# Loading the first two row tiles of x as one transfer, with the third on another queue and one short warming matmul less

## The chip, the cores and the metric

The kernel runs on one core of one Trainium2 chip. The metric is the device time of one execution in microseconds (us), and the median of several runs is compared. Three runs of the kernel before gave 220.68, 220.12 and 220.95 us: a median of 220.68.

## The reference

One layer norm feeds two blocks that are added to the input: a linear attention with a softmax feature map (32 heads of 16), and a gated unit with a plain product.

```python
x  = A_x                                   # 2048 x 512, bf16
xn = layernorm(x)                          # no gain, no bias
# block A
q, k, v = heads(xn @ A_wqkv)               # 32 heads of 16
phi(t)  = concat(softmax(t @ w_phi), softmax(-(t @ w_phi)))
kv, z   = phi(k)^T v, sum over rows of phi(k)
a = (phi(q) kv) / (phi(q) z + 1e-6) @ A_wo
# block B
h = (xn @ B_w_gate) * (xn @ B_w_up)        # 2048 x 1792
b = h @ B_w_down
out = x + a + b
```

## The kernel before

The 2048 rows are cut into 16 tiles of 128 rows; `xall` holds all of them, 512 columns each. `xnT` is the normalised x with its columns on the partitions, as TensorE wants it for every product that follows. The weights stay in SBUF: `wv` (the v part of `A_wqkv`, loaded in two halves), `wg` and `wu` (gate and up, loaded in column stretches), `wT2` (the k and q parts, transposed by the transfer), `wd`, `wo`.

The order of the work on each engine is the order in which the code is written; no scheduler changes it. So each engine's list and each queue's list of transfers can be read off the code:

- SyncE's queue starts with x tile 0 (L82), x tile 2 (L83) and the second half of `wv` (L84). Then come the first columns of `wg` and `wu` (L94), `wphi`, more of `wg` and `wu`, the transposing load of `wT2` and the rest.
- ScalarE's queue carries x tile 1 (L91) and the first half of `wv` (L92). GpSimd's carries x tile 3 (L93).
- Transfers from SyncE and ScalarE signal on eight semaphores in turn, and a transfer that comes round to a semaphore again waits until the transfer that used it last has landed.

The first four tiles have a path of their own, since nothing can run before them (L376 to L405). For tile 0, VectorE sums the rows (`sum_of(0)`, L374); for tiles 1 and 2 ScalarE does it with an accumulating pass into `junk` (L378); for tile 3 VectorE again. `sub_sum` (L338) makes 512 x minus the row sum on VectorE, for tile 0 in two halves, and calls it `xn`. `lt` (L206, L207) transposes `xn` by four TensorE matmuls against the identity, into a PSUM tile `tp`, and copies it to `xnT` on VectorE or ScalarE. `first_v` (L237) multiplies with `wv`; its results for tiles 0 and 1 go to `kv` banks, those of tiles 2 and 3 to `pv`. The scale by the standard deviation is applied later, when PSUM is read (L364, L362), from statistics that VectorE takes after the sums (L154, L343).

Behind that, TensorE alternates between units of the gated block (`ffn`: four matmuls `g`, four `u`), the k, q and v projections, the attention's products and the last product `fin`. Ahead of it all, TensorE runs matmuls on a constant that nobody reads, `warm_up`: seven of 512 columns (L312) and two of 128 columns (L313).

Of the kernel before, what the change touches and what calls it, by code (L numbers as in the profile page):

```python
# [21 lines left out]
def kernel(  # L22
# [12 lines left out]
    nc = tc.nc  # L35
# [32 lines left out]
    def dma_x(lo, hi, eng=nc.sync):  # L68
        eng.dma_start(out=xall[:, lo:hi, :], in_=x_view[:, lo:hi, :])
# [4 lines left out]
    def dma_wv(lo, hi, eng):  # L74
        eng.dma_start(out=wv[:, lo:hi, :],
                      in_=A_wqkv[lo * P:hi * P, 2 * D:3 * D].rearrange("(c p) f -> p c f", p=P))
# [2 lines left out]
        dma_cols(nc.sync, wg, B_w_gate, lo, hi)  # L79
        dma_cols(nc.sync, wu, B_w_up, lo, hi)  # L80

    dma_x(0, 1)  # L82
    dma_x(2, 3)  # L83
    dma_wv(2, DC, nc.sync)  # L84

    ET = mybir.EngineType
# [1 line left out]
    ones = nc.const_aps.tensor(1.0, [P, P], BF16)  # L88
    first = consts.tile([P, 1], BF16)
    nc.scalar.activation(out=first[:], in_=ones[:, 0:1], func=AF.Exp, scale=1.0)  # L90
    dma_x(1, 2, nc.scalar)  # L91
    dma_wv(0, 2, nc.scalar)  # L92
    dma_x(3, 4, nc.gpsimd)  # L93
    dma_gu(0, 2 * P)  # L94
# [212 lines left out]
    def warm_up(k, reps=DC):  # L307
        for _ in range(k):
            nc.tensor.matmul(warm[:, 0:reps * P], lhsT=ones,
                             rhs=nc.const_aps.tensor(1.0, [P, reps * P], BF16), start=True, stop=True)  # L310

    warm_up(7)  # L312
    warm_up(2, 1)  # L313

    with tc.tile_pool(name="ps_k", bufs=1, space=PSUM) as ps_k:
        kvbank = [ps_k.tile([P, TT], F32, name=f"kv{b}") for b in range(2)]
# [209 lines left out]
```

## Time and profile before

| | us |
|---|---|
| median of the three runs | 220.68 |
| lowest, highest run | 220.12, 220.95 |
| the profiled execution | 220.46 |
| its span | 218.8 |
| TensorE busy in the span | 214.9 |
| VectorE busy | 141.0 |
| ScalarE busy | 89.2 |
| GpSimd busy | 74.9 |

The span runs from the profile's first event to its last; the profiled execution took 1.66 us more than its span. Times inside the span below are counted from its start. In a timeline row the first number is the start, the second the length of the row, in us; rows of like instructions are merged, with their count after the x, and PEld is TensorE's weight load. A matmul's length contains the way through the array and overlaps with the next one's, so the pace of TensorE is read from the distance between starts. In the rows of transfers the last number is the time from the issue to the landing.

### The profile page before, as it was taken

The numbers are of one execution on the slowest core, as the hardware profiler recorded it, in microseconds if no ns is written. First come the engines' busy times: TensorE is split into PE (matmuls) and PEld (weight loads), VectorE is DVE, ScalarE is ACT, GpSimd is POOL, SyncE is SP. The second block draws the span as 40 slices with busy tenths as digits, with TensorE's granted clock in tenths as the row PEclk, the third lists the DMA queues.
The fourth block names the chain that finished last, engine by engine and source line by source line (L and its number), as shares of the span: only waits on it lengthen the run. The fifth ranks groups of instructions, "written<-read, shape, count | busy, mean of one in ns | idle before, by whom it ended". The sixth has DMA issues, their size and how long they took to land.

```text
span 218.8 us, 3493 instructions
## 1 busy us (share of the span) xinstructions
PE 214.9 (98%) x1291; PEld 103.1 (47%) x1291; DVE 141.0 (64%) x242; ACT 89.2 (41%) x159; POOL 74.9 (34%) x72
## 2 busy tenths in 40 slices
PE   8999999999999999999999999999999999999994
PEld 3444445454444444444544444444444444454443
DVE  4878867786598758576599773296655655454321
ACT  5545686569575875565435212141231322100000
POOL 4450843373357554636045333033123033000000
PEclk9999999999999999999999999999999999999999
DMA  5999996005202240202028355114461431412201
GB/s 198 286 297 372 372 219 136 2 0 51 48 0 49 51 94 2 48 3 48 1 43 105 76 114 114 37 24 96 96 70 30 95 72 28 96 48 72 69 30 48
DMA packets 48433, 19.91 MB, mean 91 GB/s; under 512 B 37504, under 2 KB 48384, under 8 KB 48416
## 3 DMA queue, kind: packets, MB, share of 16 engines
q1 hardware_dynamic: 47952, 19.16, 38.9%
q10 hardware_dynamic: 416, 0.39, 0.5%
q8 instruction: 10, 0.16, 0.3%
q0 software_dynamic: 48, 0.13, 0.2%
q14 instruction: 7, 0.06, 0.1%
HBM read 8.67 MB, written 2.10 MB: 49 GB/s over the span
## 4 chain that ended last, share of the span: by engine, by line
PE 97%; DMA 1%; DVE 1%; issue 0%
PE g L275 22%; PE fin L291 22%; PE u L279 22%; PE fin L294 6%; PE q L237 6%; PE k L237 6%; PE pv L237 6%; PE kv L331 2%; PE ab L465 2%; DMA xall<-in_A_x_dram 1%; PE kv L237 1%; PE tp L206 1%; PE pq L226 1%; DVE tot L374 0%; DVE xn L338 0%; DVE o_sb L301 0%
## 5 line engine op out<-in xcount | busy, mean ns | idle before, releaser
L275 PE MATMUL g<-xnT,wg 128*128 128x512 bf16 x224 | 57.5, 379 | 0.0
L279 PE MATMUL u<-xnT,wu 128*128 128x512 bf16 x224 | 57.5, 379 | 0.0
L254 POOL TENSOR_TENSOR phiq<-e,rsum 128x1024 bf16<-128x1024 f32 x16 | 30.9, 1933 | 63.5 <-DVE rsum L252 56.0
L283 DVE TENSOR_TENSOR hT<-u,g_sb 128x512 bf16<-128x512 f32 x56 | 37.0, 666 | 23.9 <-PE u L279 15.8
L282 ACT CAST g_sb<-g 128x512 bf16<-128x512 f32 x56 | 32.9, 587 | 46.8 <-PE g L275 46.5
L250 DVE TENSOR_REDUCE sums<-e 128x64 f32<-128x1024 f32 x32 | 38.9, 1216 | 20.1 <-ACT e L247 20.1
L291 PE MATMUL fin<-wd,hT 128*128 128x512 bf16 (+2 forms) x238 | 51.1, 366 | 0.0
L254 POOL TENSOR_TENSOR phik<-e,rsum 128x1024 bf16<-128x1024 f32 x16 | 30.9, 1932 | 39.6 <-DVE rsum L252 33.6
L279 PEld LDWEIGHTS <-wu 128*128 128x128 bf16 x224 | 21.9, 98 | 26.4
L291 PEld LDWEIGHTS <-hT 128*128 128x128 bf16 x238 | 22.4, 98 | 24.8
L275 PEld LDWEIGHTS <-wg 128*128 128x128 bf16 x224 | 21.1, 98 | 24.0
L237 PEld LDWEIGHTS <-xnT 128*128 128x128 bf16 x192 | 17.4, 98 | 18.2 <-ACT xnT L207 0.7
L301 DVE TENSOR_TENSOR o_sb<-fin,xall 128x512 bf16<-128x512 f32 (+2 forms) x13 | 8.5, 651 | 20.5 <-PE fin L294 20.5
L252 DVE RECIPROCAL rsum<-sums 128x64 f32<-128x64 f32 x32 | 17.7, 553 | 3.1
L294 PE MATMUL fin<-wo,oT 128*128 128x512 bf16 (+2 forms) x68 | 16.6, 366 | 0.0
L237 PE MATMUL k<-W1k,xnT 128*128 128x512 bf16 x64 | 16.4, 379 | 0.0
L237 PE MATMUL q<-W1q,xnT 128*128 128x512 bf16 x64 | 16.4, 378 | 0.0
L246 ACT ACTIVATE e<-q 128x512 f32<-128x512 f32 x12 | 7.2, 597 | 22.2 <-PE q L237 22.2
L237 PE MATMUL pv<-wv,xnT 128*128 128x512 bf16 x56 | 14.4, 379 | 0.0
L478 DVE TENSOR_TENSOR otok<-ab,rden 128x512 bf16<-128x512 f32 x16 | 11.1, 692 | 0.6
L323 ACT CAST vt<-pv 128x512 bf16<-128x512 f32 x12 | 7.0, 587 | 10.0 <-PE pv L237 10.0
L154 DVE BATCH_NORM_STATS2 stats<-xall 128x6 f32<-128x512 bf16 x16 | 10.6, 664 | 0.0
(63 smaller groups left out, 131.8 us busy)
## 6 DMA issues: line engine op xcount, KB each, us to landing
out_dram<-o_sb SPq DMA_DIRECT2D x15, 128.0 KB, 2.0
wd<-in_B_w_down_dram SPq DMA_DIRECT2D x1, 1792.0 KB, 15.8
xall<-in_A_x_dram SPq DMA_DIRECT2D x1, 1024.0 KB, 11.9
wg<-in_B_w_gate_dram SPq DMA_DIRECT2D x1, 640.0 KB, 7.7
wu<-in_B_w_up_dram SPq DMA_DIRECT2D x1, 640.0 KB, 10.4
xall<-in_A_x_dram SPq DMA_DIRECT2D x1, 512.0 KB, 4.5
wg<-in_B_w_gate_dram SPq DMA_DIRECT2D x1, 512.0 KB, 5.3
wu<-in_B_w_up_dram SPq DMA_DIRECT2D x1, 512.0 KB, 6.4
```

The lines of the kernel that those rows point to most:

```text
L154: nc.vector.bn_stats(out=stats[:], in_=xall[:, n, :])
L237: nc.tensor.matmul(ps, lhsT=xnT[:, j, n * P:(n + 1) * P], rhs=w[:, j, :], start=(j == 0), stop=(j == DC - 1))
L250: nc.vector.tensor_reduce(out=sums[:], in_=ev, axis=AX.X, op=ALU.add)
L252: nc.vector.reciprocal(out=rsum[:].rearrange("p a b -> p (a b)"), in_=sums[:])
L254: nc.gpsimd.tensor_tensor(out=phi[:].rearrange("p g (x f) -> p (g x) f", f=DH), in0=ev, in1=rsum[:].to_broadcast((P, 2 * H, DH)), op=ALU.mult)
L275: nc.tensor.matmul(gps, lhsT=wg[:, c, f * P:(f + 1) * P], rhs=xnT[:, c, T * TT:(T + 1) * TT], start=(c == 0), stop=(c == DC - 1))
L279: nc.tensor.matmul(ups, lhsT=wu[:, c, f * P:(f + 1) * P], rhs=xnT[:, c, T * TT:(T + 1) * TT], start=(c == 0), stop=(c == DC - 1))
L282: nc.scalar.copy(out=g_sb[:], in_=gps)
L283: nc.vector.tensor_tensor(out=hTs[T][:, f, :], in0=ups, in1=g_sb[:], op=ALU.mult)
L291: nc.tensor.matmul(ps, lhsT=hTs[T][:, f, t4 * P:(t4 + 1) * P], rhs=wd[:, f, lo:lo + w], start=(f == 0), stop=False)
L294: nc.tensor.matmul(ps, lhsT=oTs[n][:, c, :], rhs=wo[:, c, lo:lo + w], start=False, stop=(c == DC - 1))
L478: nc.vector.tensor_tensor(out=o_tok[:].rearrange("p (b h d) -> p b h d", b=2, d=DH), in0=abv[:, :, :, 0:DH], in1=rden[:].to_broadcast((P, ...
```

## The change

x tiles 0 and 1 are asked for by one instruction on SyncE's queue (256 KB in place of 128 KB), tile 2 moves from SyncE's queue to ScalarE's, into the place that tile 1 had there, and the second of the two short warming matmuls is dropped. Lines from 84 on move up by one.

```diff
@@ -79,8 +79,7 @@
-    dma_x(0, 1)
-    dma_x(2, 3)
+    dma_x(0, 2)
     dma_wv(2, DC, nc.sync)
@@ -88,7 +87,7 @@
     nc.scalar.activation(out=first[:], in_=ones[:, 0:1], func=AF.Exp, scale=1.0)
-    dma_x(1, 2, nc.scalar)
+    dma_x(2, 3, nc.scalar)
     dma_wv(0, 2, nc.scalar)
     dma_x(3, 4, nc.gpsimd)
@@ -310,7 +309,7 @@
     warm_up(7)
-    warm_up(2, 1)
+    warm_up(1, 1)
```

Nothing else moves: each compute engine's list is as before, but for the one warming matmul and its weight load on TensorE. Both the sum of tile 0 on VectorE and the sum of tile 1 on ScalarE now wait for the one transfer. There is one transfer less in the turn of the eight semaphores, so every later transfer on SyncE's queue waits for another one than before.

## The prediction

> **What bounds the kernel now.** I read the page first (busy times, the slices, the chain's shares), then the chain of waits in order of time, then the timeline of the first 6 us, then the rows of transfers.
>
> The page's busy times, the granted clock in slices, and the chain's shares:
>
> ```profile
> PE 214.9 (98%) x1291; PEld 103.1 (47%) x1291; DVE 141.0 (64%) x242; ACT 89.2 (41%) x159; POOL 74.9 (34%) x72
> ...
> PEclk9999999999999999999999999999999999999999
> ...
> PE 97%; DMA 1%; DVE 1%; issue 0%
> ```
>
> TensorE (PE) is the bound, and 97% of the chain that ends last is its own work. The change touches none of that work, only when it starts. So the head of the chain decides (start, length, what):
>
> ```profile
> 0.79 2.45 DMA xall<-in_A_x_dram
> 3.25 0.02 issue
> 3.27 0.70 DVE tot L374
> 3.97 0.03 issue
> 3.99 0.30 DVE xn L338
> 4.29 0.05 issue
> 4.34 1.07 PE tp L206 x8
> 5.40 0.54 PE kv L237 x2
> 5.94 0.22 PE tp L206 x4
> ```
>
> The reader is to see that tile 0's landing at 0.79 + 2.45 = 3.24 sets the first real TensorE instruction at 4.34: 1.10 us of sum, subtraction and hand-overs lie between. From 4.34 on the chain never leaves TensorE again until the last output.
>
> The timeline of the same stretch, and of the issue queues:
>
> ```profile
> 0.83 3.36 PE L309 MATMUL warm<-const-bfloat16-1.0 128*128 128x512 bf16 x9 [0.83 <-PEq L510]
> 0.85 0.40 ACTq L69 DMA_DIRECT2D xall<-in_A_x_dram  x1
> 1.28 0.45 ACTq L75 DMA_DIRECT2D wv<-in_A_wqkv_dram  x1
> ...
> 3.57 0.63 ACT L378 ACTIVATE junk<-xall 128x512 bf16<-128x512 bf16 x1 [1.28 <-DMA xall<-in_A_x_dram]
> 3.77 0.15 PEld L309 LDWEIGHTS <-const-bfloat16-1.0 128*128 128x128 bf16 x1 [0.28 <-issue]
> ...
> 3.99 0.75 DVE L338 TENSOR_SCALAR xn<-xall,tot 128x256 bf16<-128x256 bf16 x3
> 4.11 0.19 ACT L378 ACTIVATION_READ_ACCUMULATOR junk<-xall 128x1 f32 x1
> ```
>
> The nine warming matmuls start 0.43 us apart when they are long and 0.11 when short; the last one starts at 3.88, so TensorE is free from 3.99 and stands idle for 0.35 us until 4.34. Two more readings of the starts matter. The eight transposes go from 4.34 to 5.20, 0.107 each, and the four at 5.78 take 0.055 each: TensorE runs at half pace at first, although the page's clock row shows full in all slices. And the first two `kv` matmuls start at 5.20 and 5.56. At 0.427 for a slow one and 0.216 for a fast one (four `g` take 0.86), a distance of 0.36 means 0.29 us of slow pace: full pace came at about 5.49, 4.66 us after the first warming matmul.
>
> **The change part by part.** *Tiles 0 and 1 in one transfer.* Its landing T isn't in the trace. The rows of transfers give the bounds:
>
> ```profile
> wv<-in_A_wqkv_dram ACTq DMA_DIRECT2D x1, 256.0 KB, 3.4
> ...
> xall<-in_A_x_dram ACTq DMA_DIRECT2D x1, 128.0 KB, 2.7
> ```
>
> From below: T is 3.24, if the second 128 KB cost nothing. From above: the first half of `wv` has the new transfer's size and shape and took 3.4 us, behind other transfers, so T = 0.79 + 3.4 = 4.19. Nearest is the pair itself: asked for at 0.79 and 0.85 on two queues, tile 1 was in when ScalarE began on it at 3.57. The same 256 KB beside the same neighbours, plus 0.03 us for the longer issue (`wv`'s 0.43 against 0.40): T = 3.60, and d = T - 3.24 = 0.36 us. A second way agrees: from 2.6 to 3.6 us all transfers together moved 343 to 379 GB/s, and 131 KB at 360 GB/s are 0.36 us.
>
> The Trainium skill ("DMA: Bandwidth & Descriptors", section "Anatomy of one DMA") fits 2.0 us plus the bytes at 436 GB/s, for GpSimd's queue. By it tile 0 alone takes 2.30 us, where the trace has 2.45, and d would be 0.30.
>
> *What tile 0's lateness does.* VectorE is the carrier: sum 3.27, the halves of tile 0's `xn` from 3.99 and 4.19, tile 1's `xn` from 4.40, then copies; these follow each other with no idle time named in the timeline. All of it moves by d, the first transpose to 4.34 + 0.36 = 4.70.
>
> *What tile 1's landing does.* It comes at 3.60 in place of 3.57. Its sum on ScalarE was ready at 4.11 + 0.19 = 4.30 and will be at 4.33; tile 1's `xn` could not start before 4.40 anyway, and now starts near 4.76. No gain, no loss: VectorE's order covers 0.43 us.
>
> *Tile 2 on ScalarE's queue* is issued at 0.85 in place of about 1.2. It lands near tile 1's old time, 3.6, in place of about 3.9. Its sum comes second on ScalarE, at 4.33 before, behind tile 1's, so it is not earlier; its `xn` stands at 5.19 in VectorE's list. Nothing, and if it were as late as 4.19 it would still be ahead of its turn. The `wv` half behind it keeps its place at 1.28 and landed at 4.68, ahead of its use at 5.20.
>
> *SyncE's queue* has one issue less of about 0.46 us. The second half of `wv` (issued 1.71, landed 4.4 later, at 6.1, needed at 6.96), `wg` (2.18 + 4.9 = 7.1, needed at 9.34) and `wu` (2.70 + 5.4 = 8.1, needed at 10.20) go out earlier and were not waited for. The waits for another semaphore in turn concern the later stretches: the second `wu` now waits for the new transfer (in by 4.19 at the latest, and it was issued at 4.36), the transposing load for `wv`'s second half, as before. GpSimd's queue isn't passed. Zero; without this cover the loss per transfer is what it comes late.
>
> *One short warming matmul less.* It frees 0.11 us of TensorE in which TensorE waits anyway: zero by itself. Together with d the idle hole grows from 0.35 us (3.99 to 4.34) to 0.82 us (3.88 to 4.70).
>
> *The sum.* From the first transpose on TensorE is the bound, so d passes to the end, but the work moved past 5.49 runs at twice the pace. Before, 4.34 to 5.49 did 1.15 us of slow work, worth 0.575 us of fast; after, 4.70 to 5.49 does 0.395. The end moves by 0.575 - 0.395 = 0.18 us. If full pace comes later by d as well, or if VectorE's shifted list (tile 2's `xn` would end at 5.53 + 0.36 = 5.89, its transpose came at 5.78) is what TensorE waits for, the end moves by all 0.36. I take 0.25, between the two, with 0 (d = 0) and 0.95 (T = 4.19, nothing regained) as ends. Against the profiled execution: 220.46 + 0.25 = 220.7. That execution lies 0.22 under the median of the runs shown, so the forecast for the median is 220.68 + 0.25 = 220.9 us.
>
> **The rivals.** *The hole keeps TensorE slow for longer* (slower). Speaking for it: full pace came only after 4.66 us of activity, and the hole in it more than doubles. Speaking against: 0.35 us of hole did no such harm. If the change of pace counts anew from the first transpose, full pace comes at 4.70 + 4.66 = 9.36. Slow work until then is worth 2.33 us of fast, and the end moves by (9.36 - 2.33) - (5.49 - 0.575) = 2.1 us: 222.6 on the profiled execution, 222.8 on the median. It decides only between 0.35 and 0.82 us of hole.
>
> On this the Trainium skill ("TensorE: Matmul & The Clock Gate", Part 1) says that half pace is the default, that one busy window of about 3.4 us ends it, and that the windows run freely, whatever the kernel does. By it a window that the larger hole spoils costs another 3.4 us at half pace, 1.7 us in the end, an estimate, and the executions scatter by as much; the three runs shown, 0.83 us apart, don't contradict it.
>
> *The second 128 KB cost nothing* (not slower). T = 3.24; for it speaks that the transfers moved only 87 to 128 GB/s before 2.4 us, so the start is latency and not rate; against it, that tile 1 on another queue came 0.33 us after tile 0. Then VectorE starts as before and nothing moves: 220.46, 220.7 on the median. It can't be faster: the earlier sum of tile 1 waits for VectorE's turn.
>
> *The merged transfer is as late as the half of `wv`.* T = 4.19, d = 0.95, first transpose at 5.29. By the sum above the end moves by 0.48 to 0.95: 221.2 to 221.6 on the median. Against it: `wv` stood behind two x tiles.
>
> **How the numbers follow.** Forecast 0.55, longer slow pace 0.24, no cost 0.11, late landing 0.10. A measurement of this kernel can tell about 0.5% from no change, 1.1 us. The forecast, no cost and late landing stay within 219.6 to 221.8; the longer slow pace lies beyond. Slower by over 0.5%: 0.27, that rival and a little of the late landing. Faster: even full pace from the first transpose at 4.34 would save only 0.575 us, so 0.04 for what I don't see. Within: 0.69. The forecast's own range is 220.4 to 221.3, a fourth of a microsecond for T and the rest for the scatter of the runs; the range goes from 220.2 into the rival's, to 222.6, which leaves out its upper half and little below.
>
> **What would show it.** The merged transfer's landing (3.6), the sum at 3.6, the first transpose at 4.7, a hole of 0.8 us ahead of it, and where the starts of matmuls go from 0.43 to 0.22 apart: near 5.5 if I am right, 8 or later for the first rival. I am wrong if the first transpose starts at 4.4 or earlier, or if TensorE stands idle later than 7 us, which would mean a transfer that I called covered.

## The result, and the profile after

| | kernel before | changed kernel |
|---|---|---|
| median of 22 runs | 220.69 us | 222.18 us |
| lowest, highest | 220.08, 222.73 | 220.75, 223.12 |
| runs above 221.8 us | 1 of 22 | 14 of 22 |
| profiled execution | 220.46 us | 222.47 us |
| its span | 218.8 us | 220.7 us |

The ratio of the times is 1.0054, with a 95% interval of 1.0033 to 1.0075: the changed kernel is slower by about half a per cent. The runs of the changed kernel fall into two groups, eight from 220.75 to 221.42 and fourteen from 221.99 to 223.12, with nothing between. The profiled execution belongs to the upper one.

The page of the changed kernel still shows TensorE as the bound. The lines are the busy times of the engines and the chain's shares by engine:

```profile
PE 214.9 (97%) x1266; PEld 103.5 (47%) x1290; DVE 141.1 (64%) x242; ACT 89.2 (40%) x159; POOL 75.0 (34%) x72
...
PE 96%; DMA 1%; issue 1%; DVE 1%
```

TensorE's busy time reads the same 214.9 us in a span that is 1.9 us longer, but the two can't be compared: this page has 1266 matmuls beside 1290 weight loads, so 24 matmuls are missing from the record, where the page of the kernel before has 1291 of each. A later profile of the changed kernel that belongs to the lower group has the same 1266 matmuls and 213.1 us. So between these two like profiles the upper one has 1.8 us more of busy time: the time lost is slow work and not waiting. The chain of waits of the changed kernel, in order of time (start, length, what), shows where that comes from in its first 10 us:

```profile
0.80 3.19 DMA xall<-in_A_x_dram
3.98 0.02 issue
4.01 0.70 DVE tot L373
4.71 0.02 issue
4.73 0.30 DVE xn L337
5.03 0.05 issue
5.07 1.07 PE tp L205 x8
6.14 0.85 PE kv L236 x2
6.99 0.43 PE tp L205 x4
7.42 0.85 PE kv L236 x2
8.27 0.85 PE pv L236 x2
9.13 0.56 PE kv L236 x2
9.69 0.22 PE tp L205 x4
9.91 0.43 PE kv L236 x2
```

Two things are to be seen. The merged transfer lands at 0.80 + 3.19 = 3.99 in place of 3.24, and the first transpose comes at 5.07 in place of 4.34, 0.73 us later. And two `kv` or `pv` matmuls take 0.85 us until 9.1, then 0.43: TensorE runs at half pace until about 9.3, where the kernel before had full pace at 5.49. The second is the larger by far. From 5.07 to 9.3 at half pace, TensorE does 2.1 us worth of fast work, so the end moves by (9.3 - 2.1) - (5.49 - 0.575) = 2.3 us by the prediction's sum; the two profiled executions lie 2.0 apart.

The timeline of the changed kernel shows the hole ahead of the first transpose (PE is TensorE; the bracket is its idle time and what ended it):

```profile
0.83 3.25 PE L308 MATMUL warm<-const-bfloat16-1.0 128*128 128x512 bf16 x8 [0.83 <-PEq L509]
...
5.07 1.07 PE L205 MATMUL tp<-ident,xn 128*128 128x128 bf16 x8 [0.99 <-DVE xn L337]
```

The bracket counts 0.99 us from the modelled end of the last warming matmul. By starts, as in the prediction, the hole goes from 3.88 to 5.07: 1.19 us. All holes below are counted by starts.

### The profile page after: what moved, and what is told of

Same layout as the page of the kernel before. It is cut to its first block, busy times and chain, and to the rows that moved or that the text cites. A ratio compares the mean times of both kernels' runs of the same rounds, so it can differ in the third digit from the quotient of the medians.

```text
span 220.7 us, 3465 instructions
## 1 busy us (share of the span) xinstructions
PE 214.9 (97%) x1266; PEld 103.5 (47%) x1290; DVE 141.1 (64%) x242; ACT 89.2 (40%) x159; POOL 75.0 (34%) x72
## 4 chain that ended last, share of the span: by engine, by line
PE 96%; DMA 1%; issue 1%; DVE 1%
PE u L278 22%; PE fin L290 22%; PE g L274 22%; PE fin L293 6%; PE q L236 6%; PE k L236 6%; PE pv L236 6%; PE ab L464 2%; PE kv L330 2%; DMA xall<-in_A_x_dram 1%; PE kv L236 1%; PE tp L205 1%; PE pq L225 1%; DVE tot L373 0%; DVE xn L337 0%
## 5 line engine op out<-in xcount | busy, mean ns | idle before, releaser
L278 PE MATMUL u<-xnT,wu 128*128 128x512 bf16 x221 | 56.8, 379 | 0.2
L274 PE MATMUL g<-xnT,wg 128*128 128x512 bf16 x213 | 56.3, 379 | 0.6
L236 PE MATMUL k<-W1k,xnT 128*128 128x512 bf16 x61 | 15.8, 379 | 0.0
L477 DVE TENSOR_TENSOR otok<-ab,rden 128x512 bf16<-128x512 f32 x16 | 11.1, 691 | 0.6
```

Source lines behind the costliest of these rows:

```text
L236: nc.tensor.matmul(ps, lhsT=xnT[:, j, n * P:(n + 1) * P], rhs=w[:, j, :], start=(j == 0), stop=(j == DC - 1))
L274: nc.tensor.matmul(gps, lhsT=wg[:, c, f * P:(f + 1) * P], rhs=xnT[:, c, T * TT:(T + 1) * TT], start=(c == 0), stop=(c == DC - 1))
L278: nc.tensor.matmul(ups, lhsT=wu[:, c, f * P:(f + 1) * P], rhs=xnT[:, c, T * TT:(T + 1) * TT], start=(c == 0), stop=(c == DC - 1))
L477: nc.vector.tensor_tensor(out=o_tok[:].rearrange("p (b h d) -> p b h d", b=2, d=DH), in0=abv[:, :, :, 0:DH], in1=rden[:].to_broadcast((P, ...
```

## The experiments

The theory after the result: the hole between the warming matmuls and the first transpose spoils the change to full pace in part of the executions, and the late landing costs little by itself. Its rivals: the late landing costs the time; the dropped warming matmul does. In each list of runs, those above 221.8 us are called the upper group; the kernel before, in its 22 runs above and beside each group of experiments, has 13 of 132 there. Kernels that were run together on one chip are told of together. The first four:

**The changed kernel with its hole filled.**

```diff
-    warm_up(1, 1)
+    warm_up(12, 1)
```

> The changed kernel with twelve short warming matmuls in place of one, so that TensorE stays busy until the first transpose at about 5.07. Theory (the hole of 1.19 us between 3.88 and 5.07 makes most executions stay at half pace until 8 us or later): the first transpose still starts near 5.05 to 5.1, full pace comes before 6.5, no execution lies at 222 or above, median 220.8 to 221.2. Rival (the late landing alone costs the time, and the hole does nothing): median 222.2, as the changed kernel, with full pace near 9 again.

Measured: median 221.22 us (220.61 to 221.64, 12 runs), none in the upper group; 220.85 for the kernel before beside it, ratio 1.0011 (0.9990 to 1.0031). Its timeline on TensorE from 3 us on:

```profile
2.49 2.77 PE L308 MATMUL warm<-const-bfloat16-1.0 128*128 128x512 bf16 x15
5.05 1.06 PE L205 MATMUL tp<-ident,xn 128*128 128x128 bf16 x8
5.90 0.89 PE L236 MATMUL kv<-wv,xnT 128*128 128x512 bf16 x2
6.63 0.39 PE L205 MATMUL tp<-ident,xn 128*128 128x128 bf16 x4
6.86 0.59 PE L236 MATMUL kv<-wv,xnT 128*128 128x512 bf16 x2
```

The first transpose is as late as in the changed kernel, 5.05, but the four transposes from 6.63 to 6.86 already go at 0.055 us each: full pace by 6.6. The late landing alone does not make the upper group. The median is at the upper edge of what was expected, 0.37 us above the kernel before.

**The hole without the late landing.**

```diff
-    warm_up(7)
+    warm_up(5)
     warm_up(2, 1)
```

> The kernel before with five long warming matmuls in place of seven: x lands as before, at 3.24, but TensorE is idle from about 3.18 to 4.34, a hole of 1.16 us. Theory (the hole): the first transpose is where it was, but part of the executions keeps half pace until 7.5 to 10 us; two groups, 220.1 to 221.0 and 221.4 to 222.6, median above 221.0. Rival (late landing alone): nothing moves, median 220.7 and all executions below 221.1.

Measured: median 222.42 us (221.37 to 224.25, 12 runs), nine of 12 in the upper group; ratio 1.0080 (1.0048 to 1.0112). This is more than the theory asked for: even the lowest run is 1.2 us above the lowest of the kernel before beside it. Its timeline on TensorE from 3 us on:

```profile
4.25 1.07 PE L206 MATMUL tp<-ident,xn 128*128 128x128 bf16 x8 [0.92 <-DVE xn L338]
6.07 1.01 PE L237 MATMUL kv<-wv,xnT 128*128 128x512 bf16 x2 [0.74 <-DMA wv<-in_A_wqkv_dram]
6.87 0.63 PE L206 MATMUL tp<-ident,xn 128*128 128x128 bf16 x4
7.30 1.06 PE L237 MATMUL kv<-wv,xnT 128*128 128x512 bf16 x2
...
9.28 0.39 PE L206 MATMUL tp<-ident,xn 128*128 128x128 bf16 x4
```

The first transpose is even earlier than in the kernel before, at 4.25, yet the transposes at 6.87 still take 0.107 each (to 7.30), and only those at 9.28 are fast. Two long warming matmuls less cost as much as the whole change in the first 22 runs (1.57 and 1.49 us in the medians). The second row has something else that the prediction denied: TensorE waits for the first half of `wv`, until 6.02 (more on it below).

**The transfers of the changed kernel alone.**

```diff
-    warm_up(1, 1)
+    warm_up(2, 1)
```

> The changed kernel with its second short warming matmul back: the transfers of the changed kernel alone, hole 1.08 us. Theory (the hole, made by the landing at 3.99): as the changed kernel, merged transfer in at about 3.99, first transpose near 5.07, two groups, median 221.7 to 222.3. Rival (the dropped warming matmul does it): median below 221.2. Rival (late landing alone): 222.2 in one group.

Measured: median 221.97 us (220.50 to 224.56), five runs from 220.50 to 221.28 and the others from 221.91 up; the ratio 1.0022 (0.9985 to 1.0060) can't be told from the kernel before. Two groups, as the changed kernel has them, so the dropped warming matmul isn't needed for them. Its profiled execution, 221.91, is in the upper group for another reason. Its chain:

```profile
1.29 5.58 DMA wv<-in_A_wqkv_dram
6.88 0.04 issue
6.92 0.59 PE kv L236 x2
7.51 0.22 PE tp L205 x4
```

The first half of `wv` landed at 6.88, 1.5 us later than in the changed kernel's own profile (1.29 + 4.1 = 5.39); the pace was full by then.

**One warming matmul less alone.**

```diff
-    warm_up(2, 1)
+    warm_up(1, 1)
```

> The kernel before with one short warming matmul less and its own transfers: hole 0.46 us in place of 0.35. Theory (the hole, and it has to be large): 220.5 to 220.9, same as before. Rival (the dropped warming matmul does it): 221.5 or above.

Measured: median 220.90 us (220.27 to 221.40, 11 runs), none in the upper group, ratio 0.9992 (0.9969 to 1.0015). As expected: a hole that is 0.1 us longer than the one of the kernel before did nothing that can be seen in 11 runs. (In its profiled execution x came early, VectorE began at 3.03, so the hole was only 0.22 us there.)

The next three ran together on another chip.

**Why the merged transfer came at 3.99: all on SyncE's queue.**

```diff
     dma_x(0, 2)
+    dma_x(2, 3)
+    dma_wv(0, 2, nc.sync)
     dma_wv(2, DC, nc.sync)
...
-    dma_x(2, 3, nc.scalar)
-    dma_wv(0, 2, nc.scalar)
```

> The changed kernel with ScalarE's queue left empty: tile 2 and the first half of wv follow the merged transfer on SyncE's queue. It settles why the merged transfer came at 3.99 and not at 3.60. Theory (the transfers of two queues take turns, so tile 2 on ScalarE's queue took bandwidth from the merged transfer): it lands at 3.3 to 3.55. Rival (256 KB in one transfer take this long by themselves): 3.75 to 4.0 as in the three runs with the merge so far. The time isn't the question, since the first half of wv comes later.

Measured: 221.18 us in the median (220.81 to 223.09, 10 runs, three in the upper group), ratio 1.0003 (0.9960 to 1.0046). The rows of its transfers (KB, us from issue to landing):

```profile
xall<-in_A_x_dram SPq DMA_DIRECT2D x1, 256.0 KB, 2.8
...
xall<-in_A_x_dram SPq DMA_DIRECT2D x1, 128.0 KB, 2.6
```

The merged transfer took 2.8 us from its issue at 0.79, and VectorE began on it at 3.63. With tile 2 on ScalarE's queue beside it, five profiled executions have VectorE begin at 4.01, 3.86, 3.78, 3.84 and 3.94. That is between the bounds of the theory and the rival, nearer the theory: without tile 2 beside it the transfer is 0.15 to 0.38 us faster, in one execution.

That execution, 223.09, is in the upper group for a third reason. Its row of the granted clock and its timeline on TensorE:

```profile
PEclk9699999999999999999999999999999999999999
...
2.49 1.39 PE L308 MATMUL warm<-const-bfloat16-1.0 128*128 128x512 bf16 x4
4.70 0.86 PE L205 MATMUL tp<-ident,xn 128*128 128x128 bf16 x8 [0.81 <-DVE xn L337]
6.55 0.65 PE L236 MATMUL kv<-wv,xnT 128*128 128x512 bf16 x2 [1.00 <-DMA wv<-in_A_wqkv_dram]
6.99 0.63 PE L205 MATMUL tp<-ident,xn 128*128 128x128 bf16 x4
7.42 1.06 PE L236 MATMUL kv<-wv,xnT 128*128 128x512 bf16 x2
...
10.39 0.59 PE L236 MATMUL kv<-wv,xnT 128*128 128x512 bf16 x2
```

By the starts, full pace came during the warming already, at 3.55. TensorE then stood idle for 0.81 us ahead of the first transpose and for 1.00 us ahead of `wv`, and at 6.97 it went back to half pace (the two `kv` from 7.42 take 1.06, those from 10.39 take 0.59) until 10.38. The clock row shows this as a 6 in its second slice, from 5.5 to 11.1 us. So full pace can also be lost again.

**A hole of the size that the prediction expected.**

```diff
-    warm_up(7)
+    warm_up(6)
     warm_up(2, 1)
```

> The kernel before with six long warming matmuls in place of seven: a hole of about 0.78 us (3.56 to 4.34), the size that the prediction expected of the change. Theory (a hole spoils the more executions, the larger it is): between the 0.46 us hole, which did nothing, and the 1.16 us hole, 222.4: median 221.0 to 221.9, with part of the executions above 221.5. Rival (a threshold between 0.8 and 1.1 us): median 220.9 and no more executions above 221.5 than the kernel before has.

Measured: median 220.90 us (220.42 to 222.93, 12 runs): seven runs from 220.42 to 220.98, five from 221.96 up; ratio 1.0008 (0.9970 to 1.0046). The median is the rival's, the five of 12 are the theory's; the kernel before had six of 29 in the upper group beside it, so the share is larger but not clear of chance. In its profiled execution, 222.93, the hole was 0.66 us, since x came a little earlier, and TensorE waited another 0.49 us for `wv`. The upper group lies where larger holes put it: its middle run is at 222.39, and the middle of the changed kernel's upper group is at 222.47.

**The kernel before with its hole filled.**

```diff
-    warm_up(2, 1)
+    warm_up(5, 1)
```

> The kernel before with five short warming matmuls in place of two, which closes its own hole of 0.35 us. Theory (a hole this small does no harm): median within 0.2 us of the kernel before; the few executions of the kernel before above 222 may vanish if they are holes' work. Rival (each bit of hole costs): median lower by 0.2 to 0.4 us, 220.5.

Measured: median 220.90 us (220.29 to 221.21, 12 runs), none in the upper group; ratio 0.9990 (0.9962 to 1.0018). The median doesn't move; no run is in the upper group, where the kernel before had six of 29 beside it (this too is not clear of chance in 12 runs).

**The first half of `wv` ahead of its second half**, on a further chip, with the hole filled and without:

```diff
     dma_x(0, 1)
-    dma_x(2, 3)
+    dma_wv(0, 2, nc.sync)
     dma_wv(2, DC, nc.sync)
...
     dma_x(1, 2, nc.scalar)
-    dma_wv(0, 2, nc.scalar)
+    dma_x(2, 3, nc.scalar)
...
-    warm_up(2, 1)
+    warm_up(5, 1)
```

> The kernel before with tile 2 and the first half of wv exchanged between the two queues (SyncE: tile 0, both halves of wv; ScalarE: tiles 1 and 2) and five short warming matmuls in place of two. The profiles so far show the first half of wv landing anywhere from 4.68 to 6.9, and TensorE waiting for it for up to 1.2 us, which the prediction called covered. Theory (its second half, on the other queue, takes turns with it; behind it in one queue it can't): it lands by 5.0, TensorE doesn't wait for it, full pace before 6.5, and the median is 0.2 to 0.5 us below the kernel before. Rival (its landing has other causes): it lands at 5.5 or later, median as the kernel before.

> As the last one, with the two short warming matmuls of the kernel before: the transfers alone. Theory (queues take turns): as the last one within 0.1 us in the median, since a hole of 0.35 us does little, but with one execution in ten or so above 222. Rival: as the kernel before.

Measured: filled 220.93 us (220.72 to 221.44, 12 runs), ratio 1.0000 (0.9987 to 1.0014); with the hole of the kernel before, 220.90 (220.66 to 223.10), two of 12 in the upper group, ratio 1.0014 (0.9988 to 1.0040). The landing came nearly as expected, at 5.25 in the filled one, where TensorE began with `wv` at 5.30, 0.1 us after its transposes. The median that was expected, 0.2 to 0.5 us below the kernel before, was missed: the gain went into the next wait. The chain of the filled one:

```profile
1.26 3.84 DMA xall<-in_A_x_dram
5.10 0.02 issue
...
5.19 0.73 ACT junk L378 x2
5.92 0.02 issue
5.94 0.36 DVE xn L338
```

Tile 2 now lands at 5.10, ScalarE sums it at 5.19, and TensorE gets its transposes at 6.35 where the kernel before had them at 5.78. What one transfer gains in this stretch, another loses.

**The changed kernel once more, beside a second way of filling its hole**, on one more chip; the diff is that of the second:

```diff
-    warm_up(7)
-    warm_up(1, 1)
+    warm_up(9)
+    warm_up(3, 1)
```

> The changed kernel as it is, beside the next one on one chip, since its first runs and those of the filled hole were not made on the same chip. Theory (the hole): more than half of the executions between 221.9 and 223.2, the others between 220.7 and 221.5. Rival (the chip made the difference between the changed kernel and the filled hole): no second group here, median below 221.5.

> The changed kernel with nine long and three short warming matmuls in place of seven and one, so that TensorE is busy until about 5.0: the hole closed with other instructions than in the first filling. Theory (the hole): no execution above 221.9, median 220.9 to 221.4, that is 0.1 to 0.5 above the kernel before, which is what the late landing costs by itself. Rival: as the changed kernel beside it.

Measured: the changed kernel 220.87 us (220.56 to 222.73, 12 runs), with a ratio of 1.0021 (0.9995 to 1.0047); three runs of 12 in the upper group, from 222.12 up. The two groups are there, but the expected share was missed: here most runs are in the lower one. Filled: 220.75 (220.68 to 221.54, 12 runs), ratio 1.0007 (0.9995 to 1.0020), none in the upper group. The profiled execution of the unfilled one, 220.58, is of the lower group. Its chain:

```profile
0.80 3.02 DMA xall<-in_A_x_dram
...
4.91 0.85 PE tp L205 x8
5.76 0.43 PE kv L236 x2
```

The same program, with nearly the same late landing (3.82), is at full pace from the first transpose on: by the starts full pace came at 3.70, in the last long warming matmul and ahead of the hole of 1.11 us, which then did no harm. It ends within 0.15 us of the kernel before's profiled execution. The share of the upper group differs from one set of runs to the next; that it comes from the hole rests on the pairs that were run together (0 of 12 filled beside seven of 12 with the merged transfers alone; nine of 12 with the hole alone beside four of 35 of the kernel before) and on the sum over all kernels, whose holes are known from one or two profiles each. With the hole filled (0 to 0.32 us left in the four profiles: two fillings of the changed kernel, two with the kernel before's first transfer) 0 of 48 runs are in it. With 0.22 to 0.53 us (the kernel before, one matmul less, `wv` first) it is 15 of 155; with 0.66 to 1.19 us (the changed kernel twice and four others) 41 of 80. Not all of the 41 need be the hole's: in one profile the late `wv` alone was enough, and in another full pace was lost again.

## Why the prediction was right or wrong

The time is inside the range, and the slowdown lies at the edge of what the prediction called measurable (0.54%, interval 0.33 to 0.75). The case that it named likeliest is the one of the lower group, 0.2 us above the kernel before (median of the eight runs 220.9, just as forecast). In the first 22 runs that was the minority; the rival at 0.24 made the median. The range held because it reached into that rival's times; the forecast value, 220.9, was missed by 1.3 us. In the 12 later runs of the same kernel it would have been met (220.87). So that the number came out as it did is in part luck: the prediction had no account of what puts an execution into one group or the other.

*The bound.* Right: 96% of the chain is TensorE's.

*The landing of the merged transfer.* Too early, and this is the term that was mis-sized: T = 3.60 and d = 0.36 were taken, 3.99 and 0.75 measured, 3.76 to 3.92 in four more executions. The step that failed is the choice of the nearest row, "the same 256 KB beside the same neighbours". The likely reason: in the kernel before, tiles 0 and 1 came in on two queues, each with its own share. In the changed one both are on one queue, and tile 2 on the other draws its share at the same time, so the merged transfer ends when nearly all three tiles are in. The row for that was in the prediction too: tile 2 at about 3.9. One execution with tile 2 out of the way gave 3.6. The Trainium skill ("DMA: Bandwidth & Descriptors", section "Issuing engines are not separate DMA queues") says that all queues end in the same 16 engines and interleave there. The one run without tile 2 beside the merged transfer agrees: 2.8 us from issue to landing, against 3.0 to 3.2 in the five profiles with it.

*What the late landing costs.* Right in size, as far as can be told: 0.25 us was taken. With the hole filled, the ratios are 1.0011 (0.9990 to 1.0031) and 1.0007 (0.9995 to 1.0020), that is 0.24 and 0.15 us of 220.8, neither of them clear of zero (0.37 and -0.01 by the medians), although d was nearly twice what was taken. Two reasons are likely and not tested apart. One is the sum's own: work that comes after the change of pace is done at twice the speed. The other is that TensorE waits for `wv` in five of the 11 experiments' profiles in any case.

*The pace.* The forecast let full pace come at 5.49 or a little later. That is the step that failed: in the profile of the upper group it came at 9.3, and the times of the other 13 runs up there lie around that one's. The rival had this, and its price, 2.1 us with full pace at 9.36, stands beside a measured 2.0 between the profiled executions with full pace at about 9.3. Its place between 0.35 and 0.82 us of hole fits the counts as well, but not as a sharp point: it is a chance that grows. Its rule, that full pace "counts anew from the first transpose", is not what the traces show: full pace came 4.2, 4.4 and 6.0 us after the first transpose in the profiles of the changed kernel, the hole alone and the middle hole, and 1.2 us ahead of it in the later profile of the changed kernel.

What the traces show in its place are stretches of 3.4 us. In the run with all on SyncE's queue, full pace lasted from 3.55 to 6.97 and half pace from there to 10.38. In the ten profiles where the starts tell when full pace came, TensorE had been idle for at most 0.8 us in the 3.4 us before, and for at least 1.16 us in the 3.4 us that came before those (the time ahead of its first instruction counted as idle). So a reading that fits them all, and that no run was made to test, is this: full pace comes at the end of a stretch of 3.4 us that was nearly all busy, a hole that falls into the wrong stretch costs another one at half pace, and where the stretches lie differs between executions of one program (3.70 and 9.27 in the two profiles of the changed kernel). It would also account for the hole alone, where every run was slower: no 3.4 us that end before about 6.8 have less than 0.8 us idle there.

The Trainium skill ("TensorE: Matmul & The Clock Gate", Part 1) has windows of about 3.4 us that run freely, of which one must be busy. The run with all on SyncE's queue agrees, with its two stretches of 3.4 us. Half of such a window is 1.7 us, an estimate from the page's figure; the two groups of the changed kernel lie 1.55 us apart in their medians (220.91 and 222.47).

*One warming matmul less.* Right: zero alone (0.9992). Here it adds 0.11 us to a hole that the transfer made.

*The covers.* For `wg`, `wu` and SyncE's later transfers, right: TensorE waited for none of them in the changed kernel's profile. For the first half of `wv`, wrong: the 4.68 of one profile (4.64 before rounding) was a lucky execution. It landed at 5.39 in the changed kernel's and at up to 6.88 in others, and TensorE waited 0.49 to 1.22 us for it in five of the 11 experiments' profiles.

*What the sources of the half per cent are.* Shown: closing the hole with the transfers left as they are removes the upper group (0 of 24 runs in two fillings, 17 of 34 unfilled), and making it with the old transfers produces that group. Not shown: how much a late `wv` adds to a large hole, since no run changes that landing there. Open: why the share was 14 of 22 in the first runs and three of 12 later; chance alone can't be ruled out.

## What to carry to other kernels

Where TensorE has still to come up to full pace, look at the distance of the starts and not at the clock row alone, and keep the warming work going until the first real instruction is certain to be ready: a short matmul too many costs 0.1 us at most, a hole can cost 2 us in some executions. When a transfer is merged with another, its landing is that of everything which the other queues deliver beside it; take the row of the last of those bytes. And a wait that one profile shows as covered by half a microsecond is not covered if the landing scatters by two: no reordering here, nor any filling, beat the kernel before in the median by more than 0.01 us, though the four filled ones had no run above 221.7 us.

## What the runs showed that was not expected

The start of this kernel has two sources of scatter of more than 1 us that one profile doesn't show. The landing of the same 256 KB of `wv`, issued at the same moment (1.28), was anywhere from 4.64 to 6.02 with the transfers of the kernel before. And the moment at which TensorE goes from half to full pace was 9.3 in one execution of the changed kernel and 3.7 in another, 1.9 us apart in the end (222.47 and 220.58). The profile's row of the granted clock showed full in all slices in both; of all the profiles here, it showed half pace only where full pace was lost again, with everything on SyncE's queue.
